# One block of a recurrent-attention and mixture-of-experts kernel: attention outputs dealt out anew over tiles and PSUM banks

## The chip, the cores and the metric

The kernel runs on one core of one Trainium2 chip. The metric is the device time of one execution in microseconds (us). The kernel before takes 883.65 us, the median of three runs (883.22 to 885.49).

## The reference, cut to what matters

Three layers follow each other. The first is a gated recurrent attention with 4 batches, 8 heads, 768 positions and 48 values per head:

```
for t in range(S):
    cur = einsum('bhd,bhe->bhde', u * k[t], v[t])
    y[t] = einsum('bhd,bhde->bhe', r[t], state + cur)
    state = w[t][..., None] * state + einsum('bhd,bhe->bhde', k[t], v[t])
```

Its output, 3072 rows of 384, goes through `a = x @ w1; b = x @ w2; x = (a * b @ w3) @ w_out` with an inner width of 1024, and then through eight experts, of which each row takes the best two by noisy gate values. All in float32.

## The kernel before, in words

**Attention in chunks.** The sequence is cut into 24 chunks of 128 positions, six to a batch (`CPB` = 6). For each chunk the state and the decays are folded so that the output is a sum of two kinds of matrix products. Within the chunk, `at_A` forms a 128x128 matrix of key-query products per head (eight products of 48x128, in two PSUM banks, called `bST`); VectorE merges them under a mask into a tile `am` (`at_ov`). The output is then value times `am`, plus, in every chunk but the first of a batch, state times query. `at_kv` forms the chunk's key-value products in the PSUM bank `bK` (columns 0 to 191); VectorE adds the carried state (`stmp`) and scales it (`snew`), ScalarE copies it into the state tile `S` that the next chunk reads.

**Outputs.** `at_y` forms the outputs of a chunk in the bank `bY`, transposed: 384 rows (8 heads of 48) as three blocks of 128 rows, each block as four pieces of 32 rows, each piece a 128x32 tile of TensorE at its own column position. A head gives one full piece of 32 and half of a second one. `PIECES` says which head or pair of heads lies in which piece. Every piece has one or two products with `am` and, after the first chunk of a batch, one with the state: 16 and 12 products. They are issued in seven rounds of four pieces. Then ScalarE copies the 128x384 result to `xh` and VectorE writes the rest, `xl`.

**What consumes it.** Two chunks make a group. Twelve sub-steps per group (`mo_ab`, `mo_x`) are the dense layer: each value is carried as a high and a low part, and each product is done three times (lines 182 to 184). The first product with `xl` of a group waits for the second chunk's `xl`. The gate of the experts works in batches of four chunks; its small products (lines 692 to 695) are written to columns 256 to 295 and 400 to 407 of `bK`.

**What sets the order.** Each step of a chunk has a slot in a list (`STEPS`, `WHEN`, `LATE`); all that has the same slot runs in the order of the list. VectorE runs in program order throughout. TensorE and ScalarE are ordered by a scheduler at first, TensorE in program order from group 2 on (chunks 6 and later are done there), ScalarE in the last group. In the first two groups the products of chunks 2 to 5 are thus placed by the scheduler, within what the waits allow.

**After attention.** From about 427 us on, the last group of the dense layer and the eight experts follow, with matmuls of 128x512, 128x288 and 128x384.

Of the kernel before, what the change touches and what calls it, by code (L numbers as in the profile page):

```python
# [16 lines left out]
OP = mybir.AluOpType  # L17

P = 128
B, H, S, D = 4, 8, 768, 48  # L20
# [3 lines left out]
CPB = S // P  # L24
# [12 lines left out]
DUMP = NT * P  # L37
NROW = N + DUMP

PIECES = (  # L40
# [3 lines left out]
)  # L44


def piece_rows(pc):
    a, b = pc
    if b is None:
        return [a * D + i for i in range(32)]  # L50
    return [a * D + 32 + i for i in range(16)] + [b * D + 32 + i for i in range(16)]


ROWMAP = np.array([r for kb in PIECES for pc in kb for r in piece_rows(pc)])
TIMES = np.concatenate([np.arange(HC)[::-1], np.arange(HC, P)])
# [16 lines left out]
def tile_kernel(ctx: ExitStack, tc: tile.TileContext, dt, nat, w3t, wout, w1, w2, e1, e2, cf, ci, out):  # L72
    nc = tc.nc
    pe, act, dve, pool, sp = nc.tensor, nc.scalar, nc.vector, nc.gpsimd, nc.sync
# [13 lines left out]
    act = Pinned()  # L88

    def f(ap):  # L90
        return ap.bitcast(F32)
# [25 lines left out]
    bA, bB, bX, bY, bST, bK = PB[0], PB[1], (PB[2], PB[3]), PB[4], (PB[5], PB[6]), PB[7]  # L117
# [18 lines left out]
    St = [att.tile([P, 4, 2 * D], F32, name=f"S{i}", bufs=1) for i in range(2)]  # L136
# [50 lines left out]
    DT, RK, VV, FG, RC, KT, RT, AM, KN, XH, XL, KS = ({} for _ in range(12))  # L187
# [17 lines left out]
    def fgv(j):  # L205
        return FG[j].rearrange("p (a i) -> p a i", i=HC + 1)
# [9 lines left out]
    def pre_rec(j, step):  # L216

        fa = fgv(j)[:, :, 1:]
        if step == 0:
            RC[j] = att.tile([P, 8, HC], F32, name="rc", bufs=1)  # L220
            KT[j] = att.tile([P, 4, 2, HC], F32, name="kt")
            act.activation(out=RC[j], in_=fa, func=AF.Ln)
            act.activation(out=RC[j], in_=RC[j], func=AF.Exp, scale=-1.0)
        else:
            t = KT[j].rearrange("p a s i -> p (a s) i")
            dve.tensor_tensor(out=t, in0=fa, in1=RC[j], op=OP.mult)
            dve.scalar_tensor_tensor(RC[j], t, -2.0, RC[j], op0=OP.add, op1=OP.mult)
# [60 lines left out]
    def vv(j, h):  # L288
        return VV[j][:, h * VW:(h + 1) * VW]

    def at_kv(j):
# [14 lines left out]
        for hb in range(2):  # L306
            q = slice(64 * hb, 64 * hb + D)
            act.copy(out=St[(j + 1) % 2][q, :, D * hb:D * hb + D], in_=new[q])

    def at_y(j):  # L310
        first = j % CPB == 0
        yv = bY[:, :3 * P].rearrange("p (k t) -> p k t", k=3)
        qs = []
        for q in range(4):
            lst = []
            for kb in range(3):
                a, b = PIECES[kb][q]
                if b is None:
                    hs, so = ((a, 32 * (a % 2)),), 64 * (a % 2)
                else:  # L320
                    hs, so = ((a, 32), (b, 0)), 32
                ms = [(vv(j, h)[:, o:o + 32], AM[j][:, h, :]) for h, o in hs]
                if not first:
                    ms.append((St[j % 2][:, a // 2, so:so + 32], RT[j][:, a // 2].rearrange("p s i -> p (s i)")))
                for i, (lt, rh) in enumerate(ms):
                    lst.append((yv[32 * q:32 * q + 32, kb], lt, rh, i == 0, i == len(ms) - 1, (0, 32 * q)))
            qs.append(lst)
        for i in range(max(map(len, qs))):
            for q in range(4):
                if i < len(qs[q]):  # L330
                    o, lt, rh, st, en, tp = qs[q][i]
                    pe.matmul(o, lt, rh, start=st, stop=en, tile_position=tp)  # L332
        g, s = divmod(j, 2)
        if s == 0:
            XH[g] = xp.tile([P, 3, 2 * P], F32R, name="xh")
            XL[g] = xp.tile([P, 3, 2 * P], F32R, name="xl")
        h, l = XH[g][:, :, s * P:s * P + P], XL[g][:, :, s * P:s * P + P]
        act.copy(out=h, in_=yv)
        dve.tensor_tensor(out=l, in0=yv, in1=f(h), op=OP.subtract)  # L339

    RD = {}

    def v_read(j):
        RD[j] = RD.get(j, 0) + 1
        if RD[j] == 1 + (j % CPB < CPB - 1) and j + 2 < NCH:
            load_v(j + 2)

    def do_y(j):
        at_y(j)
        v_read(j)  # L350

    def do_u(j):
# [21 lines left out]
    def do_r(j):  # L374
        pre_r(j)
        if j + 2 < NCH:
            load_dt(j + 2)

    STEPS = (do_kv, do_y, at_A, do_ov, do_T, pre_scan, lambda j: pre_rec(j, 1), pre_k, do_r, lambda j: pre_rec(j, 0),
             do_u, pre_c, pre_d, do_half)  # L380


# [84 lines left out]
    def at(slot, fn, *a):  # L467
        todo.setdefault(slot, []).append((fn, a))
# [31 lines left out]
    for k, slot in WLD.items():  # L500
        at(slot, load_w, *k)
    for i, fn in enumerate(STEPS):
        for j in range(NCH):
            late = 3 if j == NCH - 1 and i == 1 else 0
            at(WHEN[j][i] if j in WHEN else 6 * j - 14 + LATE[i] - late, fn, j)
# [388 lines left out]
    first = True  # L894
# [111 lines left out]
    for g in range(NGRP):  # L1006
# [15 lines left out]
        for i in range(12):  # L1022
# [8 lines left out]
            k = SPG * g + i  # L1031
# [99 lines left out]
    first = False  # L1131
# [122 lines left out]
```

## Time and profile before

| | |
|---|---|
| median of 3 runs | 883.65 us |
| profiled execution, its own time | 885.03 us |
| its span | 883.2 us |
| TensorE matmul busy | 868.2 us, 98% of the span |
| VectorE, ScalarE, GpSimd busy | 56%, 49%, 28% |
| chain that ended last | TensorE 90%, VectorE 6%, ScalarE 2% |
| granted TensorE clock | 90% or more of full speed in every slice |
| `am` products of `at_y` (line 332) | 768 records, 34.9 us busy |
| state products of `at_y` (line 332) | 480 records, 29.3 us busy |
| `at_A` (line 263) | 384 records, 29.9 us busy |

A float32 matmul stands in the trace as two records, so the 28 products of a chunk are 56 records. Busy times of tiles that run side by side are added up as the union of their spans, and matmuls are pipelined: what a step costs TensorE is read from start to start, not from the duration of one record. A square bracket behind a row names the idle time before it and what ended it.

### The profile page before, as it was taken

The numbers are of one execution on the slowest core, as the hardware profiler recorded it, in microseconds if no ns is written. First come the engines' busy times: TensorE is split into PE (matmuls) and PEld (weight loads), VectorE is DVE, ScalarE is ACT, GpSimd is POOL, SyncE is SP. The second block draws the span as 40 slices with busy tenths as digits, with TensorE's granted clock in tenths as the row PEclk, the third lists the DMA queues.
The fourth block names the chain that finished last, engine by engine and source line by source line (L and its number), as shares of the span: only waits on it lengthen the run. The fifth ranks groups of instructions, "written<-read, shape, count | busy, mean of one in ns | idle before, by whom it ended". The sixth has DMA issues, their size and how long they took to land.

```text
span 883.2 us, 18271 instructions
## 1 busy us (share of the span) xinstructions
PE 868.2 (98%) x7333; PEld 808.3 (92%) x7333; DVE 497.3 (56%) x1215; ACT 435.0 (49%) x876; POOL 243.9 (28%) x216
## 2 busy tenths in 40 slices
PE   8999999999999999999999999999999999999996
PEld 6789899999999999999999989899998998989896
DVE  6899875856756756765475453352534434343430
ACT  5777666566466456555454343433433344343431
POOL 2010021041141141232344343407052260613113
PEclk9999999999999999999999999999999999999999
DMA  9955399556467464433266587829368392854213
GB/s 348 390 207 208 97 128 264 134 172 191 118 202 186 133 177 128 98 120 122 69 190 130 157 252 200 210 59 239 84 181 186 93 217 63 242 121 102 27 13 48
DMA packets 123968, 139.22 MB, mean 158 GB/s; under 512 B 74977, under 2 KB 103649, under 8 KB 123873
## 3 DMA queue, kind: packets, MB, share of 16 engines
q1 hardware_dynamic: 100336, 109.58, 43.0%
q0 software_dynamic: 12160, 19.72, 11.6%
q10 hardware_dynamic: 11376, 8.65, 3.0%
q8 instruction: 59, 0.97, 0.5%
q14 instruction: 37, 0.30, 0.1%
HBM read 88.12 MB, written 36.04 MB: 141 GB/s over the span
## 4 chain that ended last, share of the span: by engine, by line
PE 90%; DVE 6%; ACT 2%; issue 1%; DMA 1%; POOL 0%; SPq 0%; POOLq 0%; DVEq 0%; ACTq 0%
PE pb L182 27%; PE pb L183 27%; PE pb L184 26%; PE pb L332 3%; PE pb L263 3%; PE pb L932 1%; PE pb L296 1%; DVE cvz L166 1%; DMA rawf<-wout 1%; DVE w3l L173 1%; ACT top L153 0%; DVE am L268 0%; DVE WAl L173 0%; DVE fg L210 0%; PE pb L412 0%
## 5 line engine op out<-in xcount | busy, mean ns | idle before, releaser
L937 POOL DMA_INDIRECT out<-ye,ti x49 | 76.7, 1565 | 225.3 <-ACT ye L927 204.8
L910 DVE SCALAR_TENSOR_TENSOR HH<-pb,HH 128x256 fp32r<-128x256 f32 (+1 forms) x128 | 71.1, 557 | 112.5 <-ACT HH L909 112.5
L182 PE MATMUL pb<-XTh,WAh 128*128 128x512 f32 (+1 forms) x384 | 131.7, 343 | 0.0
L184 PE MATMUL pb<-XTh,WAl 128*128 128x512 f32 (+1 forms) x384 | 131.4, 342 | 0.0
L183 PE MATMUL pb<-XTl,WAh 128*128 128x512 f32 (+1 forms) x384 | 131.0, 341 | 0.0
L182 PE MATMUL pb<-WBh,HH 128*128 128x384 f32 x384 | 129.3, 337 | 0.0
L184 PE MATMUL pb<-WBh,HH 128*128 128x384 f32 x384 | 128.4, 334 | 0.0
L183 PE MATMUL pb<-WBl,HH 128*128 128x384 f32 x384 | 128.4, 334 | 0.0
L909 ACT ACTIVATE HH<-pb 128x256 fp32r<-128x256 f32 (+1 forms) x128 | 62.7, 491 | 115.6 <-PE pb L184 113.4
L742 POOL DMA_INDIRECT slots<-g_sc,g_si x48 | 51.5, 1073 | 127.5 <-DVE g_si L741 71.9
L927 ACT ACTIVATE ye<-pb,ti 128x384 f32<-128x384 f32 x42 | 24.4, 582 | 124.2 <-PE pb L184 124.2
L183 PE MATMUL pb<-xl,WAh 128*128 128x256 f32 x288 | 80.9, 281 | 0.8 <-DVE xl L339 0.8
L182 PE MATMUL pb<-xh,WAh 128*128 128x256 f32 x288 | 81.5, 284 | 0.0
L183 PE MATMUL pb<-xl,WBh 128*128 128x256 f32 x288 | 81.1, 281 | 0.0
L182 PE MATMUL pb<-xh,WBh 128*128 128x256 f32 x288 | 81.0, 281 | 0.0
L184 PE MATMUL pb<-xh,WBl 128*128 128x256 f32 x288 | 81.0, 281 | 0.0
L184 PE MATMUL pb<-xh,WAl 128*128 128x256 f32 x288 | 80.8, 281 | 0.0
L183 PEld LDWEIGHTS pb<-XTl,WAh 128*128 128x128 f32 x384 | 72.3, 188 | 7.5
L184 PEld LDWEIGHTS pb<-XTh,WAl 128*128 128x128 f32 x384 | 72.2, 188 | 7.5
L182 PEld LDWEIGHTS pb<-XTh,WAh 128*128 128x128 f32 x384 | 72.0, 188 | 7.5
L182 PEld LDWEIGHTS pb<-WBh,HH 128*128 128x128 f32 x384 | 72.1, 188 | 5.0 <-ACT WAh L810 4.4
L243 POOL TENSOR_TENSOR rku<-nrk 128x384 f32<-128x384 f32 x21 | 21.3, 1012 | 196.5 <-DVE cc L250 80.8
(203 smaller groups left out, 2069.1 us busy)
## 6 DMA issues: line engine op xcount, KB each, us to landing
dtc<-dt SPq DMA_DIRECT2D x24, 772.0 KB, 5.1
raw<-e SPq DMA_DIRECT2D x18, 768.0 KB, 6.1
raww<-e SPq DMA_DIRECT2D x14, 768.0 KB, 5.0
nrk<-nat SPq DMA_DIRECT2D x24, 384.0 KB, 5.9
expert_rows<-xg SPq DMA_DIRECT2D x45, 192.0 KB, 4.4
rawf<-w3t SPq DMA_DIRECT2D x16, 512.0 KB, 7.2
nv<-nat SPq DMA_DIRECT2D x24, 256.0 KB, 4.5
out<-zeros SPq DMA_DIRECT2D x9, 576.0 KB, 3.7
```

The source lines that it names most:

```text
L166: dve.scalar_tensor_tensor(z, mid, 13, t, op0=OP.logical_shift_right, op1=OP.bitwise_or)
L182: pin(pe.matmul(o, wh, xh, start=start, stop=False))
L183: pe.matmul(o, wh, xl, start=False, stop=False)
L184: pe.matmul(o, wl, xh, start=False, stop=stop)
L243: on.tensor_tensor(out=t, in0=RK[j][:, :DM], in1=RK[j][:, DM:], op=OP.mult)
L263: pe.matmul(bST[hb][:, P * a:P * a + P], KT[j][q, a].rearrange("p s i -> p (s i)"), RT[j][q, a].rearrange("p s i -> p (s i)"), start=True, ...
L332: pe.matmul(o, lt, rh, start=st, stop=en, tile_position=tp)
L742: ins = pool.indirect_dma_start(out=table, out_offset=bass.IndirectOffsetOnAxis(ap=si[:, i, k:k + 1], axis=0), in_=SC[:, i, k, :], in_offs ...
L909: act.activation(out=Hh[hf][:, ff], in_=bank[:, :n], func=AF.Relu)
L910: dve.scalar_tensor_tensor(Hl[hf][:, ff], bank[:, :n], 0.0, f(Hh[hf][:, ff]), op0=OP.max, op1=OP.subtract)
L927: act.activation(out=y[:n], in_=bank[:n], func=AF.Copy, scale=wt)
L937: ins = pool.indirect_dma_start(out=out, out_offset=bass.IndirectOffsetOnAxis(ap=ti(e, j)[:, 0:1], axis=0), in_=y[:n], in_offset=None, com ...
```

## The change

The pieces are dealt out so that block 0 holds the four pairs of half heads (2q and 2q+1), block 1 the full pieces of the even heads and block 2 those of the odd heads. Blocks 0 and 1 stay in `bY`; block 2 goes to columns 256 to 383 of `bK`. State products of block 0 still run over 128 rows, since two heads share a piece; those of blocks 1 and 2 run over the 48 rows of a single head, as tiles of 48x32: even heads at rows 0 to 47, odd heads at rows 64 to 111. The four of block 1 and the four of block 2 alternate, in different banks. The step is cut in two: `at_y` does the `am` products of blocks 0 and 1 and the state products of block 0, `at_y2` comes after `at_A` in the list and does the `am` products of block 2, the eight single-head state products and the evacuation. The evacuation to `xh` and `xl` is two copies and two subtractions per chunk, one for the 256 columns in `bY` and one for the 128 in `bK`. The host lays the dense layer's weights out by `PIECES`, so nothing else moves.

```diff
-PIECES = (
-    ((0, None), (1, None), (0, 1), (6, None)),
-    ((2, None), (2, 3), (3, None), (7, None)),
-    ((4, 5), (4, None), (5, None), (6, 7)),
-)
+PIECES = tuple(tuple(row(a) for a in range(0, 8, 2)) for row in
+               (lambda a: (a, a + 1), lambda a: (a, None), lambda a: (a + 1, None)))
...
+    def y_bank(kb):
+        return bK[:, 2 * P:3 * P] if kb == 2 else bY[:, P * kb:P * kb + P]
+
+    def av(j, kb, q, i, stop):
+        h, o = ((2 * q, 32), (2 * q + 1, 0))[i] if kb == 0 else (2 * q + kb - 1, 32 * (kb - 1))
+        pe.matmul(y_bank(kb)[32 * q:32 * q + 32], vv(j, h)[:, o:o + 32], AM[j][:, h, :],
+                  start=i == 0, stop=stop, tile_position=(0, 32 * q))
+
+    def rs(j, kb, q):
+        r, so = (slice(0, P), slice(0, D), slice(64, 64 + D))[kb], (32, 0, 64)[kb]
+        pe.matmul(y_bank(kb)[32 * q:32 * q + 32], St[j % 2][r, q, so:so + 32],
+                  RT[j][r, q].rearrange("p s i -> p (s i)"), start=False, stop=True, tile_position=(r.start, 32 * q))
...
+        for i in range(2):
+            for q in range(4):
+                av(j, 0, q, i, first and i == 1)
+        if not first:
+            for q in range(4):
+                rs(j, 0, q)
         for q in range(4):
...
+            av(j, 1, q, 0, first)
+
+    def at_y2(j):
+        first = j % CPB == 0
+        for q in range(4):
+            av(j, 2, q, 0, first)
+        if not first:
             for q in range(4):
...
+                for kb in (1, 2):
+                    rs(j, kb, q)
...
-        h, l = XH[g][:, :, s * P:s * P + P], XL[g][:, :, s * P:s * P + P]
-        act.copy(out=h, in_=yv)
-        dve.tensor_tensor(out=l, in0=yv, in1=f(h), op=OP.subtract)
+        for k, src in ((slice(0, 2), bY[:, :2 * P].rearrange("p (k t) -> p k t", k=2)), (2, y_bank(2))):
+            h, l = XH[g][:, k, s * P:s * P + P], XL[g][:, k, s * P:s * P + P]
+            act.copy(out=h, in_=src)
+            dve.tensor_tensor(out=l, in0=src, in1=f(h), op=OP.subtract)
...
-    STEPS = (do_kv, do_y, at_A, do_ov, do_T, pre_scan, lambda j: pre_rec(j, 1), pre_k, do_r, lambda j: pre_rec(j, 0),
+    STEPS = (do_kv, at_y, at_A, do_y2, do_ov, do_T, pre_scan, lambda j: pre_rec(j, 1), pre_k, do_r, lambda j: pre_rec(j, 0),
...
+        i = 1 if fn == do_y2 else i - (i > 3)
```

How this moves the instructions is shown at three places, as the built programs have them. Line numbers of the changed kernel are its own (its lines 179 to 181 are lines 182 to 184 of before, 260 is 263, 270 is 273, 293 is 296, 700 to 703 are 692 to 695). `pb_76` is the bank `bY`, `pb_79` is `bK`, `pb_77` and `pb_78` are the two banks of `at_A`; `am` and `nv` are the merged matrix and the values, `rt` and `S_...` the query and the state, `kn` the keys turned round. What stands in square brackets is the engine or the DMA queue whose count the instruction waits for.

TensorE in chunk 8 of before, in the middle of the run: the end of `at_y`, and `at_A` of the next chunk.

```order
L332 MATMUL pb_76<-rt,S_109 32x128 x2
L332 MATMUL pb_76<-am,nv 32x128 x5
L332 MATMUL pb_76<-rt,S_109 32x128 x4
L263 MATMUL pb_77<-rt,kt 128x128 [waits DVE_49]
L263 MATMUL pb_78<-rt,kt 128x128
```

The same place in the changed kernel.

```order
L312 MATMUL pb_76<-am,nv 32x128 x4
L260 MATMUL pb_77<-rt,kt 128x128 [waits DVE_49]
L260 MATMUL pb_78<-rt,kt 128x128
L260 MATMUL pb_77<-rt,kt 128x128
L260 MATMUL pb_78<-rt,kt 128x128
L260 MATMUL pb_77<-rt,kt 128x128
L260 MATMUL pb_78<-rt,kt 128x128
L260 MATMUL pb_77<-rt,kt 128x128
L260 MATMUL pb_78<-rt,kt 128x128
L312 MATMUL pb_79<-am,nv 32x128 [waits DVE_49]
L312 MATMUL pb_79<-am,nv 32x128 x3
L317 MATMUL pb_76<-rt,S_109 32x128
```

The `am` products of block 2 have moved behind `at_A` and wait for VectorE, which reads the key-value products of the same bank; the eight state products follow, bank by bank in turn.

TensorE in before around the key-value products of chunk 2 (written to `pb_79`), which the scheduler had put far ahead of the outputs of that chunk.

```order
L184 MATMUL pb_75<-W0h,pl 128x400
L296 MATMUL pb_79<-nv,kn 32x48 [waits DMAHW1_49,Activation_49]
L296 MATMUL pb_79<-nv,kn 32x48 x15
L182 MATMUL pb_72<-xh,WAh 128x256
```

The same products in the changed kernel: they stand between the transposes of chunk 3 (line 270) and directly ahead of the key-value products of chunk 3.

```order
L270 MATMUL pb_76<-cft,kt 128x128 [waits DVE_49]
L270 MATMUL pb_76<-cft,kt 128x128 x2
L293 MATMUL pb_79<-nv,kn 32x48 [waits DVE_49]
L293 MATMUL pb_79<-nv,kn 32x48 x15
L270 MATMUL pb_76<-cft,kt 128x128
L293 MATMUL pb_79<-nv,kn 32x48 [waits DMAHW6_49,DVE_49,Activation_49]
L293 MATMUL pb_79<-nv,kn 32x48 x15
```

They now wait for VectorE, which has to read the output of chunk 2 out of the same bank first; chunk 2's slot for its output (8.25) lies ahead of that for its key-value products (8.3), and so do those of chunk 4 (16 and 17).

TensorE in before at the end of the outputs of the last chunk, 23: the small gate products that follow (lines 692 and 693) write the bank `pb_79`, where no output lies.

```order
L332 MATMUL pb_76<-rt,S_110 32x128 x4
L692 LDWEIGHTS trib
L692 MATMUL pb_79<-g_mb,trib 128x32 [waits DVE_49]
L693 LDWEIGHTS oneb
L693 MATMUL pb_79<-g_cm,oneb 128x32 [waits DVE_49]
```

The same place in the changed kernel.

```order
L317 MATMUL pb_79<-rt,S_110 32x128
L700 LDWEIGHTS trib
L700 MATMUL pb_79<-g_mb,trib 128x32 [waits DVE_49]
L701 LDWEIGHTS oneb
L701 MATMUL pb_79<-g_cm,oneb 128x32
```

The gate products write columns 256 on of the bank in which block 2 was just formed; the second of them has no wait of its own any more, since the first now waits for something later on VectorE.

## Rows read from the trace of the kernel before

**Rows 1.** The page: the costly groups, here the first products with `xl`

```profile
L183 PE MATMUL pb<-xl,WAh 128*128 128x256 f32 x288 | 80.9, 281 | 0.8 <-DVE xl L339 0.8
```

**Rows 2.** Stretches: us, then busy us (instructions) of PE, PEld, DVE, ACT, POOL

```profile
112.00:427.00 315.00, 315.00 (x3768) 304.86 (x3766) 207.97 (x601) 181.76 (x389) 78.68 (x76) 1.00 0.58 156
```

**Rows 3.** Chain of waits, chunk 10: start us, us on the chain, what

```profile
215.04 1.53 PE pb L332 x56
216.57 1.09 PE pb L263 x16
```

**Rows 4.** Chain of waits, chunk 12, the first of a batch

```profile
247.25 0.87 PE pb L332 x32
```

**Rows 5.** Instructions in order, PE, chunk 10: start us, us, engine, line, out<-in, records

```profile
214.16 0.28 PE L183 MATMUL pb<-xl,WBh 128*128 128x256 f32 x1
214.28 0.28 PE L184 MATMUL pb<-xh,WBl 128*128 128x256 f32 x1
214.49 0.55 PE L296 MATMUL pb<-nv,kn 128*32 128x48 f32 x32
...
216.17 0.40 PE L332 MATMUL pb<-rt,S 128*32 128x128 f32 x8
216.50 1.16 PE L263 MATMUL pb<-rt,kt 48*128 48x128 f32 x16
217.59 0.45 PE L182 MATMUL pb<-W0h,ph 128*128 128x400 f32 x1
217.88 0.34 PE L183 MATMUL pb<-W0l,ph 128*128 128x400 f32 x1
```

**Rows 6.** Instructions in order, DVE, chunks 2 and 3

```profile
100.15 0.56 DVE L339 TENSOR_TENSOR xl<-pb,xh 128x384 fp32r<-128x384 f32 x1 [2.28 <-ACT xh L86]
100.62 0.35 DVE L303 TENSOR_TENSOR stmp<-pb,snew 128x192 f32<-128x192 f32 x1
...
105.05 0.35 DVE L303 TENSOR_TENSOR stmp<-pb,snew 128x192 f32<-128x192 f32 x1
...
105.71 0.55 DVE L339 TENSOR_TENSOR xl<-pb,xh 128x384 fp32r<-128x384 f32 x1
106.18 1.23 DVE L210 TENSOR_TENSOR_SCAN fg<-dtc,d 128x520 f32<-128x520 f32 x1
...
110.03 0.42 DVE L231 TENSOR_TENSOR kt<-dtc,fg 128x256 f32<-128x256 f32 x1
...
111.04 0.42 DVE L238 TENSOR_TENSOR rt<-dtc,fg 128x256 f32<-128x256 f32 x1
```

**Rows 7.** The same stretch, PE

```profile
100.76 0.66 PE L273 MATMUL pb<-cft,kt 128*128 128x128 f32 x4 [0.25 <-DVE xl L339]
102.09 0.55 PE L296 MATMUL pb<-nv,kn 128*32 128x48 f32 x32 [0.68 <-ACT kn L275]
...
111.51 0.71 PE L263 MATMUL pb<-rt,kt 48*128 48x128 f32 x8 [0.34 <-DVE rt L238]
```

**Rows 8.** The same stretch, ACT

```profile
105.83 0.71 ACT L308 COPY S<-snew 48x192 f32<-48x192 f32 x2
```

**Rows 9.** Instructions in order, PE, key-value products of chunk 4

```profile
122.98 0.55 PE L296 MATMUL pb<-nv,kn 128*32 128x48 f32 x32
```

**Rows 10.** Instructions in order, DVE, output of chunk 4

```profile
123.16 0.56 DVE L339 TENSOR_TENSOR xl<-pb,xh 128x384 fp32r<-128x384 f32 x1 [2.81 <-ACT xh L338]
```

**Rows 11.** Instructions in order, PE, chunk 22

```profile
407.63 0.40 PE L332 MATMUL pb<-am,nv 128*32 128x128 f32 x8
```

**Rows 12.** Instructions in order, DVE, chunk 22

```profile
409.74 0.35 DVE L303 TENSOR_TENSOR stmp<-pb,snew 128x192 f32<-128x192 f32 x1
```

**Rows 13.** Instructions in order, PE, chunk 23 and the gate products

```profile
418.67 0.19 PE L692 MATMUL pb<-g_mb,trib 128*128 128x32 bf16 x1
```

**Rows 14.** Instructions in order, ACT, chunk 23

```profile
419.57 0.47 ACT L338 CAST xh<-pb 128x384 fp32r<-128x384 f32 x1
```

**Rows 15.** Instructions in order, DVE, chunk 23

```profile
420.07 0.56 DVE L339 TENSOR_TENSOR xl<-pb,xh 128x384 fp32r<-128x384 f32 x1 [1.07 <-ACT xh L338]
```

More of the change, by code (lines that the diff above doesn't have):

```diff
@@ L308, in at_kv @@
             act.copy(out=St[(j + 1) % 2][q, :, D * hb:D * hb + D], in_=new[q])
+    def y_bank(kb):
[8 more added lines that the diff above has]
+                  RT[j][r, q].rearrange("p s i -> p (s i)"), start=False, stop=True, tile_position=(r.start, 32 * q))
     def at_y(j):
         first = j % CPB == 0
-        yv = bY[:, :3 * P].rearrange("p (k t) -> p k t", k=3)
-        qs = []
-        for q in range(4):
[L315 to L328, printed above, removed]
+        for i in range(2):
[4 more added lines that the diff above has]
+                rs(j, 0, q)
+        for q in range(4):
+            av(j, 1, q, 0, first)
[4 more added lines that the diff above has]
+        if not first:
             for q in range(4):
-                if i < len(qs[q]):
-                    o, lt, rh, st, en, tp = qs[q][i]
-                    pe.matmul(o, lt, rh, start=st, stop=en, tile_position=tp)
+                for kb in (1, 2):
+                    rs(j, kb, q)
         g, s = divmod(j, 2)
@@ L346, in v_read, with do_y2 @@
             load_v(j + 2)
-    def do_y(j):
-        at_y(j)
+    def do_y2(j):
+        at_y2(j)
         v_read(j)
```

## The prediction

> **What bounds the kernel now.** I read the busy times by stretches first. Between 112 and 427 us, where the outputs of chunks 4 to 23 are formed, TensorE is busy for all of the stretch [rows 2]: whatever TensorE does there beyond the dense layer is paid in full, and so is every wait put on it. Then I read the page's costly groups for TensorE's waits: the dense layer waits for an output of attention once, 0.8 us for `xl` [rows 1], early, in the first group. So the outputs cost TensorE's own time and hardly any waiting. The third view is the order of instructions in the stretches where attention's chain is tight. Between 100 and 112 us VectorE works without a gap from `xl` of chunk 2 at 100.15 to `rt` at 111.04 [rows 6], and TensorE is the one that waits: 0.34 us for that `rt` before `at_A` at 111.51 [rows 7]. That stretch is bound by VectorE, and a wait put on VectorE there is paid in full too.
>
> **The round that goes.** A chunk's 28 products take 1.53 us on the chain [rows 3], 16 products without the state 0.87 [rows 4]. The difference, 0.66 us, is three rounds of four state products: 0.22 us a round. The change does blocks 1 and 2 of the state products as eight tiles of 48x32 at two row positions. If two row positions stream side by side, that is one round in place of two: -0.22 us in each of the 20 chunks with state. `at_A` shows that they do: its eight products, at two row positions in two banks, take 1.09 us [rows 3], that is four pairs of some 0.22 each plus what it costs to enter it.
>
> **The switches that come.** TensorE changes between tile shapes, and each change shows. From 256 columns of 128x128 tiles to 128x32 the starts lie 0.21 us apart (214.28 to 214.49), against 0.12 between two products of the same shape [rows 5]: 0.09 lost. At `at_A` the last two passes of the outputs start from 216.17 on, 0.11 apart, so the last at 216.28, and `at_A` at 216.50: 0.22 against 0.11, so 0.11 lost. From `at_A` into the dense layer the first product starts at 217.59 and the second 0.29 later, where 0.18 is usual for that shape [rows 5]: on top of the change itself, about 0.10 goes for a weight load of 128 columns that nothing hides. For 32 columns that part is small: 32 records of key-value products take 0.37 us (214.49 to 214.86) for eight passes of some 0.04, so about 0.02. A change into 32-column tiles thus costs 0.09 to 0.11 plus 0.02: 0.12 us. Before, a chunk has three changes (into 128x32, into `at_A`, out). After, `at_A` stands between the two halves of the outputs and the state tiles have a shape of their own: 128x32, `at_A`, 128x32, 64x32, out. Two more changes: +0.24 us.
> The change from 128x32 to 64x32 is not in the trace. Its bounds are nothing (same columns) and 0.21 (as into 128-column tiles, 0.11 plus 0.10); I take 0.12, as the nearest rows are those into 32 columns. The Trainium skill, "TensorEngine Tiling (Array Packing)", section "Key Properties", says that changing the tiling mode, not only the tile, drains TensorE. By that rule this change of shape costs a drain like the others, and the sum stays as it is; without it one could hope for nothing.
> Sum for a chunk with state and `at_A` behind it: -0.22 + 0.24 = +0.02 us; 15 such chunks from chunk 4 to 21: +0.3. The first chunks of a batch have no state round to save and one change more, three of them on the path: +0.36. So the saving itself comes to about +0.7 us, bounds -3.9 (both new changes free in 15 chunks and 3) and +4.0 (each 0.21: 0.20 x 15 + 3 x 0.21 = 3.6, rounded up for chunks 0 to 3).
>
> **Evacuation.** One subtraction of 384 columns takes 0.56 us; the next instruction starts 0.47 after it [rows 6]. Two of 256 and 128: 256 columns take 0.42 and the next starts 0.34 later (line 231, [rows 6]); 128 I estimate at 0.28, from 0.35 at 192 and 0.42 at 256. Together 0.62: +0.06 us on VectorE. ScalarE alike. It counts where `xl` is late: twice before 70 us (chunk 0, and chunk 1 where TensorE waits [rows 1]): +0.1. From 112 us on VectorE is busy for 208 of 315 us [rows 2], which hides it and the later `xl`, since `at_A` and 0.7 us of products now stand between; if that cover were gone it would cost some 0.8 us in a group.
>
> **The bank, chunks 2 and 3.** Block 2 lies in the bank of the key-value products. In chunk 2 output comes first, so its key-value products now wait until VectorE has read block 2. They used to be done at 90 us; now they stand behind `xl`, and VectorE's next instruction, `stmp`, waits for them. `xl` ends at 100.71 [rows 6]; the transposes before them (three of four, 0.13 apart) have been let go by then, the change of shape and 0.55 us of products [rows 7] follow: done about 101.6, where `stmp` began at 100.62. VectorE is late by 1.0 us. Behind it on VectorE all of the chain waits, and `stmp` of chunk 3 moves from 105.05 to 106.05 [rows 6]. The second half of chunk 3's outputs now waits for that `stmp` (same bank): it starts at about 106.5 and is done some 0.8 us later. ScalarE can copy block 2 only behind the two copies of the state, which move with VectorE from 105.83 to 106.85 and take 0.71 [rows 8]: 107.55. A copy of 0.3 and the subtraction of 0.28 end near 108.2; the scan that began at 106.18 [rows 6] begins near 108.1. So +1.95 us at `at_A` of chunk 4, which waits for this chain [rows 7]. Bounds: 0, if ScalarE and VectorE had slack there that I can't see, and 2.4.
>
> **The bank, chunk 4.** Same order of slots. The key-value products at 122.98 [rows 9] must wait for `xl`, which ends at 123.72 [rows 10], 0.06 later by the split, and its signal (some 0.05, as from the end of `xl` at 100.71 [rows 6] to the transposes at 100.76 [rows 7]): 123.83. +0.85 us on TensorE, where the dense layer is queued behind. Bounds 0 and 0.9.
>
> **The bank, chunks 6 to 22.** Here the key-value products come first, and block 2 waits for VectorE's read of them. In the middle of the run `at_A` hides it: block 2 starts 2 us after the outputs do. In chunk 22 VectorE is behind: outputs start at 407.63 [rows 11], block 2 would start at 407.63 + 0.87 + 0.1 + 1.09 = 409.7; `stmp` runs from 409.74 to 410.09 [rows 12]. +0.45 us.
>
> **The bank, chunk 23.** The gate products, at 418.67 right behind the last outputs [rows 13], write the very columns of block 2. They must wait until it is evacuated. ScalarE begins at 419.57 [rows 14], since it first has another copy to do; `xl` runs from 420.07 to 420.63 [rows 15], with the split to about 420.65. So 420.7 in place of 418.67, +2.03 us, with the whole dense layer queued behind on TensorE. The 0.45 of chunk 22 is swallowed by this wait (VectorE's part here does not move with TensorE), so both together are +2.03. Bounds 1.2 (ScalarE earlier) and 2.4.
>
> **Sum.** 0.7 + 0.1 + 1.95 + 0.85 + 2.03 = +5.6 us on the profiled execution's 885.03, of which 883.2 is span: 890.6. That execution lies 1.4 us above the median of 883.65; on the median the forecast is 889.2 us.
>
> **Rivals.**
> A. The early waits are absorbed (2.8 us of them in a stretch the scheduler orders): 889.2 - 2.8 = 886.4. For it: VectorE idles 2.28 us before `xl` of chunk 2 [rows 6]. Against: nothing idles between there and `at_A`.
> B. The eight products don't run side by side: the change doesn't do what it says, and 0.22 x 20 = 4.4 us come on top: 893.6. Against: `at_A`'s pairs [rows 3]. For: no tile of 48x32, and no eight at a time, stands in the trace.
> C. The other side, not slower: going from one tile shape of 32 columns to another, or out of `at_A`, costs nothing, because only 128-column loads show. Then 0.24 falls away in 15 chunks and 0.12 in three: 4.0 us, 885.2, which can't be told from no change. It decides from about 0.11 a change down. Against: the change into 32 columns costs 0.09 [rows 5].
> D. C and A together: 882.4 and, if the gate products also found their bank free, 880.4.
>
> **Chances.** What this measurement can tell from no change is 0.3%, 2.65 us: slower is above 886.3, faster below 881.0. The forecast has 0.58, A 0.15 (half of it under 886.3), B 0.12, C 0.10, D 0.05. Slower: 0.56 + 0.08 + 0.12 = 0.76. Faster: 0.05, with D and what I overlook. Same: 0.19. The forecast's own range is 887 to 891.5. The range for 8 in 10 takes in C's side by half and most of A, and leaves out B: 885.0 to 892.5.
>
> **What would show it.** Right: the first gate product behind chunk 23 waits near 2 us for VectorE; `stmp` of chunk 2 waits for the key-value products; the chunk from its outputs to the dense layer takes about as long as before, 2.6 us [rows 3]; eight state records start within 0.06 us and the whole round takes 0.22. Wrong: if that chunk is shorter by 0.2 us, the changes of shape are cheap (C); if longer by 0.2, the eight don't overlap (B); if the gate products don't wait, the biggest single term is gone.

## The result, and the profile after

The changed kernel takes 890.83 us (median of 6 runs, 888.97 to 892.05), the kernel before 884.0 us beside it (6 runs). The ratio is 1.0072, with a 95% interval of 1.0061 to 1.0082: slower by 6.4 us by the ratio, by 6.8 us from median to median. Its profiled execution took 890.63 us, span 888.8, against 885.03 and 883.2 before: +5.6.

To see where, I took the same instruction in both profiles (the first product of `xh` and `WAh` of each group, and others between) and subtracted the start times. What grows from one to the next was lost in that stretch:

| stretch (us, kernel before) | lost | predicted |
|---|---|---|
| start to 68.7, before the first dense product with `xh` | -2.89 | +0.1 |
| 68.7 to 113.4: chunks 2 and 3 | +1.57 | +1.95 |
| 113.4 to 123.5: chunk 4 | +1.28 | +0.85 |
| 123.5 to 403: the middle | +1.53 | +0.66 |
| chunk 22 | +2.07 | (0.45) |
| chunk 23, gate products | +1.17 | 2.03 with chunk 22 |
| 427 to the end | +0.94 | 0 |

The first and the last line lie outside the stretches in which the outputs of chunks 2 to 23 are formed; experiment 4 asks whether they belong to the change. The five between sum to 7.62 us. That the profile's own +5.6 is the sum that was forecast is therefore partly luck.

TensorE in the changed kernel, in order, at chunk 10 (start us, us, engine, line, out<-in, tile, shape, records); it answers to [rows 3, 5]:

```profile
214.85 0.55 PE L293 MATMUL pb<-nv,kn 128*32 128x48 f32 x32
215.22 0.62 PE L312 MATMUL pb<-am,nv 128*32 128x128 f32 x16
215.65 0.40 PE L317 MATMUL pb<-rt,S 128*32 128x128 f32 x8
215.87 0.40 PE L312 MATMUL pb<-am,nv 128*32 128x128 f32 x8
216.20 1.16 PE L260 MATMUL pb<-rt,kt 48*128 48x128 f32 x16
217.29 0.43 PE L312 MATMUL pb<-am,nv 128*32 128x128 f32 x8
217.65 0.45 PE L317 MATMUL pb<-rt,S 48*32 48x128 f32 x16
218.03 0.45 PE L179 MATMUL pb<-W0h,ph 128*128 128x400 f32 x1
```

From the key-value products to the dense layer 3.18 us, where [rows 5] has 3.10 (214.49 to 217.59). The eight 48x32 products (16 records, two passes) start 6.6 ns apart in the trace, the first pass within 0.05 us: they do overlap.

VectorE at chunks 2 and 3, against [rows 6]:

```profile
97.30 0.62 DVE L346 TENSOR_TENSOR xl<-pb,xh 128x256 fp32r<-128x256 f32 x2 [2.17 <-ACT xh L83]
98.87 0.36 DVE L300 TENSOR_TENSOR stmp<-pb,snew 128x192 f32<-128x192 f32 x1 [0.95 <-PE pb L293]
...
105.17 0.29 DVE L346 TENSOR_TENSOR xl<-pb,xh 128x128 fp32r<-128x128 f32 x1 [0.77 <-ACT xh L345]
...
110.24 0.42 DVE L235 TENSOR_TENSOR rt<-dtc,fg 128x256 f32<-128x256 f32 x1
```

And TensorE from there to chunk 4, against [rows 7, 9]:

```profile
97.78 0.55 PE L270 MATMUL pb<-cft,kt 128*128 128x128 f32 x3 [0.41 <-DVE xl L346]
98.26 0.55 PE L293 MATMUL pb<-nv,kn 128*32 128x48 f32 x32
...
110.72 1.16 PE L260 MATMUL pb<-rt,kt 48*128 48x128 f32 x16 [0.31 <-DVE rt L235]
...
118.55 1.16 PE L260 MATMUL pb<-rt,kt 48*128 48x128 f32 x16 [0.73 <-DVE rt L235]
...
122.94 0.55 PE L293 MATMUL pb<-nv,kn 128*32 128x48 f32 x32
```

`stmp` of chunk 2 stands behind the key-value products, and VectorE idles 0.95 us ahead of it and 0.77 us ahead of the second piece of `xl`: the two waits that were forecast. `at_A` of chunk 4, at 110.72 us here and at 111.51 in [rows 7], comes 2.10 us late when the 2.89 us are taken off by which this profile was ahead at 68.7 us; 1.95 was forecast. The dense layer behind it loses less (1.57 us), since three products that stood behind this `at_A` before, two of the dense layer and a transpose, stand ahead of it now. Not forecast is the 0.73 us at 118.55: `at_A` now comes after half of chunk 4's outputs, and `rt` (from 118.08 to 118.50) is not there yet. Before, three rounds more stood ahead of it.

The list of waits of TensorE, whole run (us in total, times, longest):

```profile
PE pb L700 <- DVE xl L346: 1.2, 1, 1.2
...
PE pb L260 <- DVE rt L235: 1.0, 2, 0.7
...
PE pb L312 <- issue: 0.7, 2, 0.3
```

The first is the gate product behind chunk 23, as forecast, 1.2 us long. The third is new: "issue" is time in which TensorE waited for nothing that the profile shows. It lies in chunk 22, shown here with the gate product behind chunk 23:

```profile
408.76 0.55 PE L293 MATMUL pb<-nv,kn 128*32 128x48 f32 x32
409.12 0.62 PE L312 MATMUL pb<-am,nv 128*32 128x128 f32 x16
409.56 0.70 PE L317 MATMUL pb<-rt,S 128*32 128x128 f32 x8
410.59 0.43 PE L312 MATMUL pb<-am,nv 128*32 128x128 f32 x5 [0.33 <-issue]
411.35 0.42 PE L312 MATMUL pb<-am,nv 128*32 128x128 f32 x3 [0.33 <-issue]
411.70 1.55 PE L260 MATMUL pb<-rt,kt 48*128 48x128 f32 x16
413.18 0.42 PE L312 MATMUL pb<-am,nv 128*32 128x128 f32 x8
...
423.40 0.18 PE L700 MATMUL pb<-g_mb,trib 128*128 128x32 bf16 x1 [1.17 <-DVE xl L346]
```

One round of four is torn apart, and `at_A` takes 1.48 us to the next row, where chunk 10 has 1.09. The gate product of [rows 13] starts 4.73 us later than before, 1.17 of them by its own wait. GpSimd beside the gaps, where it gathers rows by indirect DMAs:

```profile
409.26 0.98 POOL L849 DMA_INDIRECT xgs<-x_rows,tf  x1 [6.33 <-ACT am L253]
410.54 0.95 POOL L849 DMA_INDIRECT xgs<-x_rows,tf  x1 [0.30 <-issue]
```

In the kernel before these two gathers ran from 404.76 to 407.01 us, ahead of the small products of chunk 22, which began at 407.26:

```profile
406.05 0.96 POOL L841 DMA_INDIRECT xgs<-x_rows,tf  x1 [0.31 <-issue]
```

```profile
407.26 0.55 PE L296 MATMUL pb<-nv,kn 128*32 128x48 f32 x32
```

The scatters that feed the gathers began at 397.99 us there and at 400.40 us here.

### The profile page after: what moved, and what is told of

Read it like the earlier page. It is cut to its first block, busy times and chain, and to the rows that moved or that the text cites. A ratio compares the mean times of both kernels' runs of the same rounds, so it can differ in the third digit from the quotient of the medians.

```text
span 888.8 us, 18318 instructions
## 1 busy us (share of the span) xinstructions
PE 872.5 (98%) x7333; PEld 803.0 (90%) x7333; DVE 496.8 (56%) x1239; ACT 436.0 (49%) x900; POOL 242.9 (27%) x216
## 4 chain that ended last, share of the span: by engine, by line
PE 88%; DVE 6%; ACT 3%; issue 1%; POOL 0%; POOLq 0%; DVEq 0%; ACTq 0%
PE pb L179 27%; PE pb L181 26%; PE pb L180 26%; PE pb L260 2%; PE pb L312 2%; PE pb L940 1%; PE pb L317 1%; PE pb L293 1%; DVE cvz L163 1%; PE pb L528 1%; DVE am L265 1%; ACT am L253 1%; ACT top L150 1%; DVE fg L207 1%; PE pb L419 1%
```

## The experiments

Each edit is made to the changed kernel, unless it says otherwise. "Lost" is read as above, against the first profile of the kernel before.

**1. Gate products one slot later.**

```
- gate_at(SPG * ((t0 + GB) // 2) + 3, t0, 1 + late,
+ gate_at(SPG * ((t0 + GB) // 2) + 3, t0, (0, 0, 1, 1, 2, 2, 3, 3, 5, 5, 5) if late else 1,
```

> Only the gate products behind chunk 23 move, one slot later, behind six dense products with ph. My theory (they waited for the evacuation of block 2 with the dense layer queued behind): the 1.2 us wait of L700 for xl goes, the rest of the kernel stays, and the time falls by 1.2 to 1.6 us against the changed kernel, to about 889.5 us (+5.1 us on the kernel before in place of +6.4). Rival (the wait only hides another lateness of VectorE, which then shows at the next product with xl): the time stays within 0.3 us of the changed kernel. The stall of chunk 22 should be the same 2 us in both views, if it is the program's own and not a mishap of one execution.

Measured: 888.75 us, ratio 1.0053 (1.0039 to 1.0067). The wait for `xl` is gone; from before chunk 23 to behind it nothing is lost (3.60 to 3.58 us; +1.17 without the edit). Chunk 22 loses 1.81 us. So the gate products' wait is paid in full by the dense layer, and the loss of chunk 22 is not a mishap of one execution, since it comes back in a second program.

**2. Key-value products of chunks 2 and 4 first.**

```
- 2: (8.3, 8.25, ...   4: (17, 16, ...
+ 2: (8.2, 8.25, ...   4: (15.9, 16, ...
```

> The key-value products of chunks 2 and 4 stand ahead of the outputs of the same chunk, so they need not wait until block 2 is read out of their bank. My theory (the bank makes them wait, and chunk 3's chain on VectorE after them): at chunk 4 the shift against the kernel before falls by 1.5 us behind chunk 3 and by a further 0.2 to 1.3 us behind chunk 4, and the time falls by 1.6 to 2.8 us, to 888.0 to 889.2 us. Rival (the early stretch is bound by the split evacuation and by at_A's wait for rt, not by the bank): the gain is under 0.6 us. Of chunk 4's 1.28 us the wait of at_A for rt (0.74 us) may well stay, since its place in the order does not change.

Measured: 890.59 us, ratio 1.0070 (1.0055 to 1.0085): no gain. Chunk 4 loses 0.43 us in place of 1.28, but chunks 2 and 3 lose 3.17 in place of 1.57. ScalarE and VectorE of this run show why:

```profile
97.28 0.71 ACT L83 COPY S<-snew 48x192 f32<-48x192 f32 x2 [3.75 <-DVE snew L301]
98.01 2.45 ACT L83 ACTIVATE am<-cft,cc 128x128 f32<-128x128 f32 x8
100.36 0.51 ACT L83 CAST xh<-pb 128x256 fp32r<-128x256 f32 x2
```

```profile
100.75 0.62 DVE L346 TENSOR_TENSOR xl<-pb,xh 128x256 fp32r<-128x256 f32 x2 [3.50 <-ACT xh L83]
```

With the key-value products early, the copies of the state come early too, and ScalarE does them ahead of `am` and `xh`, which VectorE waits for (3.50 us, 2.17 without the edit). In chunk 2 the edit moved a step that I had not counted. In chunk 4 the loss fell, but the key-value products now stand where `at_A` waited for `rt` (0.73 us, 0.25 in this run), so the fall does not show that their own wait for the bank was the loss.

**3. State products of blocks 1 and 2 over all rows.**

```
- r, so = (slice(0, P), slice(0, D), slice(64, 64 + D))[kb], (32, 0, 64)[kb]
+ r, so = slice(0, P), (32, 0, 64)[kb]
...
-            for q in range(4):
-                for kb in (1, 2):
+            for kb in (1, 2):
+                for q in range(4):
                     rs(j, kb, q)
```

> Blocks 1 and 2 of the state products run over all 128 rows again (the other head's rows of the state are zeros, so the result is the same), as two rounds of four tiles of 128x32; the split in halves with at_A between, the two banks and the evacuation stay. One round more and no 64x32 shape. My theory (a round is 0.22 us, a change of shape about 0.11 us): +0.10 us a chunk with state, 20 chunks, +2 us against the changed kernel, about 892.8 us. Rival 1 (the eight tiles run one after another): no change, 890.8 us. Rival 2 (the change of shape to 64x32 costs nothing): +0.22 us a chunk, +4.4 us, 895.2 us. Rival 3 (the round of eight costs as much in its issue and its drain as the round it saves): -0.5 to +0.5 us.

Measured: 891.23 us, ratio 1.0078 (1.0063 to 1.0092). A chunk with state loses 0.135 us against the kernel before, 0.08 in the changed kernel: the round of eight is worth 0.055, half of what I put down. The time is only 0.4 us above the changed kernel's, where 2 us were expected: from 123 to 403 us 0.75 us more are lost, but chunk 22 loses 0.75 us in place of 2.07, and its small products overlap with a gather for 0.61 us only. So the stretches decide here, not the whole time. TensorE at chunk 10 of this run:

```profile
219.52 0.42 PE L312 MATMUL pb<-am,nv 128*32 128x128 f32 x8
219.76 0.62 PE L317 MATMUL pb<-rt,S 128*32 128x128 f32 x16
220.31 0.45 PE L179 MATMUL pb<-W0h,ph 128*128 128x400 f32 x1
```

Into the state products 0.24 us, here without a change of shape, 0.36 with one (217.29 to 217.65): the change costs 0.12, as put down. From there to the dense layer 0.55 with two rounds of four, 0.38 with one of eight: the round saves 0.17, not 0.22, if the step out into the dense layer costs the same from either shape. That the eight run one after another (no gain at all over two rounds) and that the change is free (0.22) are both out.

**4. The kernel before, again.**

> The kernel before, unchanged, for a second profile. If the 2.8 us by which the changed kernel was ahead at 68 us, before any output of attention, and the 0.86 us that it lost between 489 and 503 us are the executions' own scatter, this profile differs from the first one of the same kernel by as much there. If they belong to the change, it agrees with the first within 0.3 us at both places.

Measured: 883.54 us in one run. Its profile is 1.48 us ahead of the first one of the same kernel at 68.7 us and then keeps step with it within 0.06 us to the end. So between these two executions the load stretch of the first 69 us differs by more than a microsecond, and nothing behind it does. In the profiles of experiments 1 to 12 without this one, the lead at that place is 0.4 to 3.4 us. Whether the changed kernels win some of it can't be told from two profiles of before. The 0.86 us that the changed kernel's profile loses between 489 and 503 us are not seen here: the two profiles of the kernel before agree there. They do not come in experiments 1 to 3 and 5 to 9 either; losses of 1.1 to 1.6 us between 455 and 503 us come in 10, 11 and 12. Their cause is open.

**5. Block 2 in the outputs' own bank.** On top of experiment 3:

```
- return bK[:, 2 * P:3 * P] if kb == 2 else bY[:, P * kb:P * kb + P]
+ return bY[:, P * kb:P * kb + P]
```

With it, block 1's state products come ahead of block 2's products with `am`.

> Block 2 lies in the outputs' own bank again, its state products run over all 128 rows in a round of their own, and it is evacuated as a piece by itself; only the halving with at_A in between stays of the change (block 1's state products now stand behind at_A, ahead of block 2). Against the full-rows run (+6.8 us on the kernel before) only the bank differs. My theory (the bank's waits cost 2.85 us at chunks 2 to 4, 1.2 us at the gate products, and with them whatever chunk 22 loses): shift from 69 to 123 us at most +0.8 us in place of +2.8, no wait of the gate products for xl, a chunk with state in the middle of the run +0.14 us as in the full-rows run, and the time 886.5 to 888 us. Rival (the early and the late loss come from the halving and the split evacuation, not from the bank): 890 us or more, the waits of chunks 2 to 4 stay.

Measured: 890.79 us, ratio 1.0066 (1.0053 to 1.0080). The gate products no longer wait (nothing lost at chunk 23, 1.13 in experiment 3), but from 69 to 123 us 2.20 us are lost (2.77 in experiment 3). So the rival is right for most of the early part. VectorE of this run at the outputs of chunks 2 and 3:

```profile
98.56 0.29 DVE L347 TENSOR_TENSOR xl<-pb,xh 128x128 fp32r<-128x128 f32 x1 [0.33 <-ACT xh L83]
...
105.01 0.29 DVE L347 TENSOR_TENSOR xl<-pb,xh 128x128 fp32r<-128x128 f32 x1 [0.74 <-ACT xh L346]
```

In the changed kernel VectorE falls 1.0 us behind in chunk 2 and 0.9 us in chunk 3; here it is 0.4 and 0.9. The bank thus explains the larger part of chunk 2. Chunk 3 loses as much without it: the second copy of ScalarE, which stands behind the two copies of the state, is what VectorE waits for. The comparison is not clean, since VectorE is 0.5 us behind already ahead of chunk 2, where the changed kernel has 0.15. At chunk 4 `at_A` waits 0.82 us for `rt` here too. Chunk 20 lost 0.66 us more than its neighbours, inside a round, beside one slot scatter of GpSimd (376.50 to 377.51 us).

**6 and 8. Both halves joined ahead of `at_A`.** Alone (8), and with the gate products later and chunk 4's key-value products first (6):

```
- STEPS = (do_kv, at_y, at_A, do_y2, do_ov, ...
+ STEPS = (do_kv, at_y, do_y2, at_A, do_ov, ...
```

> Three edits: the second half of the outputs stands right behind the first, ahead of at_A, so that a chunk has one change of shape less; the key-value products of chunk 4 stand ahead of its outputs; the gate products behind chunk 23 come one slot later. My theory (a change of shape 0.11 us; block 2 then waits some 0.07 us for stmp, which in chunk 10 ends at 215.99 us, where the first half is done at 215.98): -0.03 to -0.10 us a chunk, the shift at 403 us against 130 us falls from +1.5 to between -0.5 and +1.0; chunk 4 -1.0; gates -1.2 to -1.7: 886 to 888 us. Rival 1 (the change of shape was never the price, the products of the second half are): the middle stays at +0.08 us a chunk, 888 us. Rival 2 (stmp is later than at_A's cover in most chunks): +0.1 us a chunk or more, over 890 us.

> Only the order of at_A and the second half of the outputs is exchanged, all else as in the changed kernel. My theory: -0.03 to -0.10 us a chunk in the middle, the wait of at_A of chunk 5 ahead of the outputs of chunk 4 gone (-0.5 us), the gate products' wait kept: 888.5 to 890.3 us. Rival (no change of shape saved, or stmp late): 891 us or more.

Measured: 887.15 us in experiment 6 (ratio 1.0034, 1.0021 to 1.0048) and 888.25 us in experiment 8 (1.0040, 1.0027 to 1.0052). TensorE at chunk 10 of experiment 8:

```profile
218.03 0.45 PE L317 MATMUL pb<-rt,S 48*32 48x128 f32 x16
218.41 1.16 PE L260 MATMUL pb<-rt,kt 48*128 48x128 f32 x16
219.50 0.45 PE L179 MATMUL pb<-W0h,ph 128*128 128x400 f32 x1
```

A chunk with state is now 0.055 us shorter than before the change, not 0.08 longer: one change of shape less is worth 0.135 us. The Trainium skill, "TensorEngine Tiling (Array Packing)", section "Key Properties", says that a change of tiling mode drains TensorE. The drain itself is not seen in the trace; a change of shape cost 0.12 to 0.14 us in these runs. The first chunks of a batch lose 0.19 us each: in chunk 6 block 2 begins at 153.32 us, when VectorE's `snew`, which reads the key-value products in the same bank, has ended (153.26).

Chunk 4 gained nothing in either run (1.25 and 1.27 us lost), so that part of the expectations failed. In 6 block 2 waits 0.61 us for `stmp` there. In 8 the key-value products wait for `xl`:

```profile
124.98 0.55 PE L293 MATMUL pb<-nv,kn 128*32 128x48 f32 x32 [0.84 <-DVE xl L346]
```

These 0.84 us are the wait that was forecast for chunk 4, 0.85. In the changed kernel TensorE has lost time by its wait for `rt` before, and only some 0.2 us are lost at the key-value products.

**7. TensorE's code shifted by 128 instructions.**

```
+    for _ in range(64):
+        tc.keep_in_program_order(pe.matmul(PB[6][:, :4], warm, warm[:, :4], start=True, stop=True))
```

> The changed kernel with 64 tiny products more at the very start (128 instructions, 8 KB of TensorE's code), to move where the code is fetched. If the 2 us that chunk 22 loses, with gaps inside a run of products that wait for nothing, come from the fetch of TensorE's code (16 KB fetched at 408.9 us, the gaps from 409.8 us), they go or move to another chunk. If they come from the work around it (the gathers of the GpSimd queue at that place), they stay within 0.5 us at the same chunk.

Measured: 889.09 us in one run. The fetch of 16 KB moves from 408.9 to 412.7 us; the gaps stay at chunk 22 (2.15 us), at 409.2, 409.9 and 410.7 us, beside gathers at 408.49 to 410.73. So it is not the place of the code.

**9. Slot scatters two slots earlier.** They feed the gathers.

```
- (13, 14, 17, 17, 19, 20, 23, 23)
+ (13, 14, 17, 17, 19, 20, 21, 21)
```

> The changed kernel; only the last two slot scatters of each gate batch but the last come two slots earlier, so that the gathers behind them (on the GpSimd queue, at 409.3 to 411.5 us in the changed kernel, 404.8 to 407.0 in the kernel before) end before chunk 22's run of small products begins. My theory (that run starves while gathers are being issued and land): the gaps of chunk 22 go, its loss falls from 2.1 us to under 0.6, and the time falls by 1.3 to 2 us against the changed kernel, to about +4.6 us on the kernel before. Rival (the gaps belong to the chunk's place, to ScalarE's table loads there or to the bank): the loss of chunk 22 stays between 0.8 and 2.1 us wherever the gathers are, and the time stays.

Measured: 895.79 us, ratio 1.0130 (1.0108 to 1.0153): slower by 5 us more. Chunk 22 lost only 0.54 us, as expected of it, since its gathers were done 0.6 us ahead of the small products. But chunks 9, 13 and 21 lost 1.75 to 1.87 us each and chunk 17 0.56, because the scatters had moved into them. GpSimd and TensorE at chunk 9:

```profile
200.61 0.96 POOL L750 DMA_INDIRECT slots<-g_sc,g_si  x1 [0.30 <-issue]
201.88 0.96 POOL L750 DMA_INDIRECT slots<-g_sc,g_si  x1 [0.30 <-issue]
```

```profile
201.50 0.39 PE L312 MATMUL pb<-am,nv 128*32 128x128 f32 x5
202.09 0.43 PE L312 MATMUL pb<-am,nv 128*32 128x128 f32 x5 [0.20 <-issue]
202.82 0.45 PE L312 MATMUL pb<-am,nv 128*32 128x128 f32 x6 [0.29 <-issue]
203.56 0.46 PE L317 MATMUL pb<-rt,S 128*32 128x128 f32 x8 [0.29 <-issue]
```

The time went the other way from what was expected, but the mechanism was made to happen at four new places: where GpSimd issues indirect DMAs beside the small products, TensorE starts them in handfuls, 0.59 to 0.74 us from one handful to the next in chunk 9.

**10. All of it combined, scatters two slots earlier.** Chunks 0 to 4 and the first of each batch are `whole`: formed in one bank at one place, over all rows, with one evacuation; the others are joined as in 8; gate products later.

```
+    def whole(j):
+        return j < 5 or j % CPB == 0
```

> Everything that the runs so far point to, in one kernel: chunks 0 to 4 and the first chunk of each batch form all three blocks in one bank at one place, as the kernel before did; the other chunks have both halves joined ahead of at_A with the round of eight; the late gate products one slot later; the slot scatters two slots earlier. My theory: no loss before 123 us (at most +0.3), -0.05 us a chunk with state to 403 us and nothing at the first chunks (-0.9 in all), chunk 22 under +0.4, chunk 23 0: 883.5 to 884.5 us, -0.1 to -0.9 us on the kernel before. Rival (the early loss comes from elsewhere, or the gaps of chunk 22 stay): 886 us or more.

Measured: 892.84 us, ratio 1.0096 (1.0078 to 1.0113). The early loss is gone (+0.05 us from 69 to 123 us), and nothing is lost at the first chunks of a batch. But chunks 9, 13, 17 and 21 lose 1.2 to 1.8 us each, by the scatters again, and chunk 22 1.6 us: with the halves joined, block 2 waits 1.46 us for a late `stmp`.

**11. Scatters one slot earlier, nothing else** (`22, 22` in place of `23, 23`).

> The changed kernel with the last two slot scatters of each gate batch but the last one slot earlier, not two: on VectorE their conversion moves from 399.98 to some 398.1 us, so that the scatters lie at some 398.5 to 401.1 us, clear of chunk 21's small products (392.5 to 395.5) and of chunk 22's (from 408.8). My theory (small products starve while GpSimd issues an indirect DMA beside them and shortly after): the gathers move from 409.3 to some 407 us or earlier, chunk 22 loses 0.5 to 1.0 us in place of 2.1, no new gap at chunks 9, 13, 17 and 21, and the time falls by 1 to 1.6 us against the changed kernel, to +4.8 to +5.4 us on the kernel before. Rival (the scatters' place in VectorE's order is what counts, not GpSimd's issue): gaps at chunks 9, 13, 17 and 21 as in the run two slots earlier, +5 us or more on the changed kernel.

Measured: 889.94 us, ratio 1.0075 (1.0061 to 1.0089): by time no gain that can be told; the profile lost 1.6 us between 455 and 503 us too. By stretches the expectation holds: no new gap, and chunk 22 lost 0.53 us. GpSimd, VectorE and TensorE there:

```profile
406.88 0.97 POOL L849 DMA_INDIRECT xgs<-x_rows,tf  x1 [5.57 <-DMA tf<-slots]
408.16 0.95 POOL L849 DMA_INDIRECT xgs<-x_rows,tf  x1 [0.31 <-issue]
```

```profile
410.94 0.35 DVE L300 TENSOR_TENSOR stmp<-pb,snew 128x192 f32<-128x192 f32 x1
```

```profile
409.81 1.16 PE L260 MATMUL pb<-rt,kt 48*128 48x128 f32 x16
411.34 0.43 PE L312 MATMUL pb<-am,nv 128*32 128x128 f32 x8 [0.37 <-DVE stmp L300]
```

The second gather still lies beside the first 0.65 us of the small products, and here no gap came of it. Without the gaps the wait for `stmp` is what is left: the chunk loses 0.53 us where 0.45 was forecast. Chunk 23 then loses 1.38.

**12. Combined, clear of the scatters.** As 10, with the scatters one slot earlier, chunks 22 and 23 whole too, and the gate products where they were.

> The combined kernel again, with the scatters one slot earlier in place of two, and with chunks 22 and 23 formed in one bank at one place like chunks 0 to 4 (so the gate products stay where they were). My theory: no loss before 123 us, -0.04 to -0.06 us at each of the 14 chunks with state that use the round of eight, no gap inside a run of small products, no wait of chunk 22 for stmp and of the gate products for xl: 0.6 to 0.9 us ahead of the kernel before by 403 us and to the end, 883.3 to 884.0 us if the kernel before has 884.4. Rival (gaps appear at other places): 885 us or more.

Measured: 882.63 us (11 runs, 881.45 to 883.57), before 884.05 (15 runs): ratio 0.9987, interval 0.9978 to 0.9996. It is ahead of both kernels. From 68.7 to 427 us it gains 0.65 us in steps of 0.04 to 0.06 at the chunks with the round of eight, and loses nothing anywhere in that stretch. Between 455 and 503 us it loses 1.1 us. So of the 1.4 us between the medians 0.65 are placed by this profile; the rest is not, and the first 69 us scatter by more than a microsecond. GpSimd and TensorE at chunk 22:

```profile
400.03 1.49 POOL L862 DMA_INDIRECT xgs<-x_rows,tf  x1 [4.04 <-ACT ph L616]
401.82 0.96 POOL L862 DMA_INDIRECT xgs<-x_rows,tf  x1 [0.30 <-issue]
```

```profile
404.04 0.55 PE L293 MATMUL pb<-nv,kn 128*32 128x48 f32 x32
...
406.05 1.16 PE L260 MATMUL pb<-rt,kt 48*128 48x128 f32 x16
```

The gathers are issued 1.3 us ahead of the small products, and no round is torn.

## Why the prediction was right, and where it was not

- **The bank at the gate products: right in kind.** 1.2 us of waiting for `xl`; experiment 1 takes it away and loses nothing at that place. With chunk 22's wait 1.91 us in experiment 11, forecast 2.03. That this wait swallows what chunk 22 loses held only for the small loss: with 1.5 us more lost there (2.07 for 0.53), the wait was but 0.2 us shorter (1.17 for 1.38), so VectorE's part did move with TensorE.
- **The bank at chunks 2 and 3: right in size, only partly the bank.** 2.10 us at `at_A` of chunk 4 for 1.95, and 1.57 in the dense layer; the waits are the ones named. But experiment 5 shows that chunk 3's part, 0.9 us, comes without the bank, by the second evacuation behind the state's copies, and experiment 10 that all of it goes when block 2's place, bank and second evacuation go together. Rival A (absorbed) is out, and with it D.
- **Chunk 4: near in size (1.28 for 0.85), another step.** I had the key-value products wait for `xl`. The 1.28 us are mainly the wait of `at_A` for `rt`, 0.73 us. I put `at_A` in the middle of the outputs and did not ask what it waits for there, three rounds (0.66 us) earlier. The forecast wait is real, 0.84 us in experiment 8, but in the changed kernel the other one hides most of it.
- **The changes of shape: right.** 0.12 and 0.135 us for two changes put at 0.12 each (experiments 3 and 8), and 0.14 us in each of the chunks 6, 12 and 18, which have one change more and no round less.
- **The round that goes: mis-sized.** Put at 0.22, it saves 0.17. So a chunk with state loses 0.08 us, not 0.02, and the middle 1.53 in place of 0.66. Rival B (not side by side) and rival C (free changes) are both out. The lower bound of the saving was added up wrongly: with both changes free, 0.22 us in 15 chunks is -3.3, not -3.9.
- **Chunk 22: a term missing.** 0.45 for `stmp` was right once the gathers are away. The other 1.5 us are gaps beside GpSimd's indirect DMAs, which lie in the run of small products since the change. I followed VectorE's and ScalarE's chains through the bank, not GpSimd's.
- **The sum.** 5.6 us forecast, 7.62 found in the stretches that the change touches; from median to median it is 6.8. In the profile the lead of the load stretch makes up for part; for the other executions that is not shown. The forecast of 889.2 us was met to 1.6 us with 2.0 us of loss missing from it, so the closeness is partly luck.

## What to carry to other kernels

A round saved by packing tiles paid here for one further change of tile shape, barely, and not for two: the round was worth 0.17 us and a change 0.12 to 0.14. A step put between two halves of another inherits an earlier due time: ask what it waits for there. When a change delays one chain, look at what the engine off the path will be doing at the new time, GpSimd too.

## What the runs showed of the hardware

In 14 profiles of this kernel and its variants, I compared each run of small products (from the key-value products to `at_A` or the last outputs) between 125 and 440 us with the times at which GpSimd issued indirect DMAs (about 1 us each). In 15 of the 16 places where the two lay beside each other for 0.74 us or more, TensorE stood idle inside the run for 0.15 to 0.33 us at a time, waiting for nothing that the profile shows (0.4 to 0.6 us from one start to the next). In the 16th, chunk 22 of experiment 2, the one idle time ends with `stmp`. Of two places with 0.61 and 0.65 us, one had such a gap; in the 250 or so with less than 0.4 us there was none. Some 420 further issues between 125 and 427 us lie beside the dense layer alone, and none of its products there starts more than 0.34 us after the one before. The runs show the coincidence and that it follows the DMAs when they are moved. What the two engines share there is not shown.
